# Leftover columns of a spectral layer as 32-row products, with its layer-norm statistics reordered

## The chip, the cores and the metric

The kernel runs on one core of a Trainium2 chip, as a single launch. The metric is device time in microseconds of that core, the median of several runs. The engines named below are TensorE (PE, with its weight loads shown as PEld), VectorE (DVE), ScalarE (ACT), GpSimd (POOL), and the DMA queues, which SyncE (SP) and POOL feed. All times are microseconds from the start of the profiled span unless marked ns.

## What is computed

The input `x` has 2048 rows of 576 columns in bf16. A spectral block is added to it, and then a gated feed-forward block:

```python
def _A_ref(x, w_r, w_i):
    B, S, D = x.shape
    X = rfft2(x.astype(float32), axes=(-2, -1))
    X = X * (w_r + 1j * w_i)
    return irfft2(X, s=(S, D), axes=(-2, -1)).astype(bfloat16)

def _B_ref(x, w_gate, w_up, w_down):
    return (gelu(x @ w_gate) * (x @ w_up)) @ w_down

x = A_x                                   # 1 x 2048 x 576
h = x + _A_ref(layernorm(x), A_w_r, A_w_i)
h2 = h + _B_ref(layernorm(h), B_w_gate, B_w_up, B_w_down)   # hidden width 4608
```

The change touches only the beginning of the spectral block: the first layer norm, and the part of the Fourier transform over rows and columns that comes first.

## The kernel before, in words

The 2048 rows stand as 16 tiles of 128 partitions (`h_sb[:, h, :]`, h from 0 to 15); row 16 p + h is partition p of tile h. The transform over the rows is split: first a product over the 128 partitions of each tile (length 128), later one that joins the 16 tiles. The transform over the columns is a product with tables of sines and cosines.

**Layer norm.** Each tile needs its mean and its 1/deviation. Eleven tiles are measured by DVE (`sd`: two `bn_stats` on halves of 288 columns, and a `bn_aggr` that joins them), five by ACT (`ln_act` on tiles 1, 3, 5, 9, 11: one pass that sums, one that sums squares, after which POOL's `ln_fin` subtracts the squared mean). POOL then makes `rstd` for groups of tiles (`ln_rstd`, L137 adds a small number, L138 raises to the power -1/2) and negative means (`minus_means`, L142, into `mneg`). DVE multiplies the row table `F16` by a tile's `rstd` (L391), which gives `FR[:, h]`. The mean is taken out by a further product with `mneg` as the weights.

**Row products.** For each tile, `row16` (L327, L334) makes six products on PE: columns 0 to 255 and 288 to 543 come out folded, that is as sums and differences of column n and column 288 + n, in a PSUM tile `f2t` that two tiles share. ACT copies it to `Bt[:, 0:4]` (`evict`, L361, one for two tiles). The columns that do not fit in these blocks, 256 to 287 and 544 to 575, are made by `rests` for four tiles at a time (`row16_rest`, L351): two products of 64 columns of `x` and two of the mean, which fill partitions 0 to 63 and 64 to 127 of one PSUM bank. Half of those 64 rows repeat columns that the blocks hold already, and the table `DF` has zeros there. `evict4` (L367) copies the bank to `Bt[:, 4]`, on ACT for tiles 0 to 7 and on DVE for 8 to 15.

**Column products.** `f2` (L550) then makes, for each of 16 groups of 128 row frequencies, six products: four with tables `DT` and two, for the leftovers, with `DF`. For the first group the two with `DF` stand last. They need all the evictions of all 16 tiles, so `f2` is the point where the opening ends. Behind it come `f3` (L567, L568), the product with the weights `WR` and `WI` on DVE, the inverse transforms (`i3`, `inv_cols`), the second layer norm, and the feed-forward block (L978 and L1021).

**The tables.** `DT` is made while the row products run: POOL makes angles (`kd`), DVE adds the phases (`phases`, L293, three of them) and drops the sign, ACT takes two sines (`col_sin`, L408), DVE mirrors them (L420) and copies rows of the third block into `DF` (L500, L501). The weights of the upper rows come by two indirect gathers on POOL (`gather`, L397) and a second transfer on SP (L504); `load_dq` (L518) rearranges `DT` into `DQ` for the inverse transform.

**Order.** Each engine works its queue strictly in the order in which the program issues; that order is written out by hand, from `for h in (1, 3, 5)` on, and no scheduler changes it. Tiles in PSUM come from one pool of four buffers of two banks that are handed round in order. Before the first row product PE multiplies an identity 12 times (`fill`, `FILL = {0: 12}`, L316), results that are overwritten. `sd` puts the `bn_aggr` of one tile between the two halves of the next (`flush`).

## Time and profile before

| What | Value |
|---|---|
| median of three runs | 494.85 us (494.26 to 495.02) |
| the profiled execution | 494.6 us, of which its span is 492.8 us |
| PE busy | 484.7 us, 98% of the span |
| DVE, ACT, POOL busy | 223.4, 158.2, 29.5 us |
| first slice of 12.3 us | PE 6 tenths, DVE 8, ACT 8, POOL 8 |
| first product of `f2` | 21.96 us |

The table of slices shows PE at nine tenths or more from the second slice to the next to last; only the first is lower. A row of the timeline reads: start, busy time from the first to the last of the merged instructions, engine, line, operation, what is written and read, shapes, and how many instructions were merged; a bracket tells how long the engine sat idle before and what released it. Busy times of matmuls include their way through the array, so products that follow each other overlap in these rows; the starts tell the pace.

### The profile page before, as it was taken

What the parts mean: (1) busy time and instruction counts of PE and PEld (TensorE: products, weight loads), DVE (VectorE), ACT (ScalarE), POOL (GpSimd) and SP (SyncE); (2) the same over time, 40 slices, a digit from 0 to 9 for tenths busy, and PEclk for the clock granted to TensorE, in tenths of its full rate; (3) what the DMA queues carried; (4) which work ended last, traced back from release to release, by engine and by line L of the source; (5) the groups of instructions that cost most, each with busy time, mean ns of one, the idle gap of its engine ahead of it and who ended that gap; (6) DMA issues with size and microseconds to landing.
All of it is one profiled execution on the core that took longest, in us unless ns stands there. A gap on an engine that the chain in (4) does not pass through costs nothing.

```text
span 492.8 us, 12868 instructions
## 1 busy us (share of the span) xinstructions
PE 484.7 (98%) x5762; PEld 338.9 (69%) x5762; DVE 223.4 (45%) x457; ACT 158.2 (32%) x280; POOL 29.5 (6%) x84
## 2 busy tenths in 40 slices
PE   6999999999999999999999999999999999999997
PEld 3777789875589955555699755555799655555995
DVE  8999774798622177333311345333121333333111
ACT  8899863322210022332200132332110232232000
POOL 8500010011100011000000000000000000000000
PEclk9999999999999999999999999999999999999999
DMA  8838979769970049966720089876600377760000
GB/s 278 234 74 184 246 115 240 165 128 212 223 161 3 3 118 195 192 145 147 152 65 1 37 170 199 174 145 147 143 3 3 92 158 155 150 146 1 14 13 25
DMA packets 89582, 62.35 MB, mean 127 GB/s; under 512 B 23222, under 2 KB 88118, under 8 KB 89526
## 3 DMA queue, kind: packets, MB, share of 16 engines
q1 hardware_dynamic: 89238, 60.34, 57.5%
q0 software_dynamic: 288, 1.18, 0.7%
q8 instruction: 45, 0.74, 0.7%
q14 instruction: 11, 0.09, 0.1%
HBM read 52.65 MB, written 2.36 MB: 112 GB/s over the span
## 4 chain that ended last, share of the span: by engine, by line
PE 95%; ACT 2%; POOL 1%; DMA 1%; issue 0%; DVE 0%; ACTq 0%; POOLq 0%
PE gu L978 57%; PE acc L1021 27%; PE pq_ps L550 2%; PE cs_ps L709 2%; PE acc L1040 2%; PE eo_ps L658 2%; ACT junk L128 1%; PE y_ps L848 1%; PE gh_ps L568 1%; PE gh_ps L567 1%; DMA h_sb<-in_A_x_dram 1%; POOL rstd L138 1%; ACT Bt L361 0%; POOL wm_r L397 0%; PE eo_ps L682 0%
## 5 line engine op out<-in xcount | busy, mean ns | idle before, releaser
L978 PE MATMUL gu<-Bt,wgu 64*128 64x512 bf16 (+1 forms) x2646 | 270.6, 363 | 0.0
L978 PEld LDWEIGHTS <-wgu 64*128 64x128 bf16 x2646 | 151.5, 94 | 115.6 <-issue 0.3
L987 DVE TENSOR_TENSOR P_sb<-g_sb,gu 128x512 bf16<-128x512 f32 (+1 forms) x156 | 100.4, 645 | 140.3 <-ACT g_sb L986 140.3
L986 ACT ACTIVATE g_sb<-gu 128x512 f32<-128x512 f32 (+1 forms) x156 | 88.0, 564 | 193.5 <-PE gu L978 193.5
L1021 PEld LDWEIGHTS <-P_sb 64*128 64x128 bf16 x2160 | 122.2, 94 | 10.9
L1021 PE MATMUL acc<-wd,P_sb 64*128 64x288 bf16 x1440 | 90.9, 283 | 0.0
L1030 DVE TENSOR_TENSOR part<-part,acc 128x576 f32<-128x576 f32 x15 | 11.3, 754 | 112.6 <-ACT part L1029 112.6
L1029 ACT COPY part<-acc 128x576 f32<-128x576 f32 x15 | 9.6, 639 | 122.8 <-PE acc L1021 122.8
L1021 PE MATMUL acc<-wd_a,P_sb 64*128 64x288 bf16 x720 | 46.8, 283 | 0.0
L550 PE MATMUL pq_ps<-DT,Bt 128*128 128x290 bf16 x64 | 12.3, 286 | 0.7 <-ACT Bt L361 0.7
L978 PE MATMUL gu<-Bt,wgu_e 64*128 64x256 bf16 (+1 forms) x162 | 12.5, 305 | 0.0
L873 DVE TENSOR_SCALAR hrow<-h_sb,mv,rstd 128x1152 bf16<-128x1152 bf16 x14 | 12.2, 868 | 0.6 <-POOL rstd L911 0.6
L138 POOL TENSOR_TENSOR rstd<-rstd,mhalf 128x1 f32<-128x1 f32 (+2 forms) x17 | 12.0, 709 | 1.4
L1032 DVE TENSOR_TENSOR h_sb<-h_sb,part 128x576 bf16<-128x576 bf16 x15 | 11.4, 758 | 0.5
L550 PEld LDWEIGHTS <-Bt 128*128 128x128 bf16 x96 | 9.1, 97 | 3.4 <-ACT Bt L361 0.8
L978 PEld LDWEIGHTS <-wgu_e 64*128 64x128 bf16 x162 | 10.3, 94 | 1.2
L137 POOL TENSOR_SCALAR rstd<-mv 128x1 f32<-128x1 f32 (+2 forms) x17 | 4.1, 242 | 116.7 <-DVE mv L123 116.0
L561 ACT CAST pq<-pq_ps 128x580 bf16<-128x580 f32 x16 | 10.5, 666 | 1.2 <-PE pq_ps L550 1.1
L709 PE MATMUL cs_ps<-DQ,EO 58*128 58x290 bf16 x144 | 10.8, 283 | 0.0
L327 PE MATMUL f2t<-FR,h_sb 128*128 128x256 bf16 x64 | 9.2, 273 | 0.6 <-DVE FR L391 0.6
L709 PEld LDWEIGHTS <-EO 58*128 58x128 bf16 x160 | 7.8, 94 | 2.4 <-issue 0.7
L550 PE MATMUL pq_ps<-DF,Bt 128*128 128x290 bf16 x32 | 8.9, 285 | 0.0
(149 smaller groups left out, 283.9 us busy)
## 6 DMA issues: line engine op xcount, KB each, us to landing
wgu<-in_B_w_gate_dram SPq DMA_DIRECT2D x46, 432.0 KB, 5.1
wgu<-in_B_w_up_dram SPq DMA_DIRECT2D x46, 432.0 KB, 6.1
wd_a<-in_B_w_down_dram SPq DMA_DIRECT2D x1, 1728.0 KB
wd<-in_B_w_down_dram SPq DMA_DIRECT2D x1, 1728.0 KB
wd<-in_B_w_down_dram SPq DMA_DIRECT2D x6, 288.0 KB, 7.9
out_dram<-h_sb SPq DMA_DIRECT2D x3, 576.0 KB
h_sb<-in_A_x_dram SPq DMA_DIRECT2D x4, 288.0 KB, 4.3
h_sb<-in_A_x_dram SPq DMA_DIRECT2D x2, 576.0 KB
```

Of the source, the lines that this page charges most:

```text
L138: G.tensor_tensor(dst[:, sl], dst[:, sl], mhalf[:, sl], ALU.pow)
L550: T.matmul(ps[:, par, 0:JP], lhsT=Bt[:, t, col], rhs=DT[:, t // 2, par] if t < 4 else DF[:, par], start=(t == par), stop=(t == 4),)
L561: copy(pq[c][:, rs].rearrange("p r (j a) -> p r j a", a=2), pq_ps[c][:, :, 0:JP].rearrange("p a (r j) -> p r j a", r=2)[:, rs],)
L658: T.matmul(pv[:, n], lhsT=z[:, a, w].rearrange("p b j -> p (b j)"), rhs=TI[:, ts[k], 1 - a : 3 - a, :], start=(a == 0), stop=(a == 1),)
L709: T.matmul(ps[:, e, 0:JP], lhsT=EO[x][rows, w, 2 * g : 2 * g + 2].rearrange("p h e k l -> p (h e k l)"), rhs=DQ[rows, w] if w or e else DT ...
L873: V.tensor_scalar(hrow[:], h_sb[:, h, :].rearrange("p (r k) -> p r k", k=64).unsqueeze(2).to_broadcast([P, NR, 2, 64]), mv2[:, h, 0:1], rs ...
L978: T.matmul(gu[:, c, 0:n], lhsT=w[rows, r, i * P : (i + 1) * P], rhs=hl[tcnk % 2][rows, r, lo:hi], start=(r == 0), stop=(r == NR - 1),)
L986: A.activation(g_sb, gu[:, 0, 0:n], ACT.Gelu_apprx_tanh)
L987: V.tensor_tensor(p_sb(f)[:, lo:hi], g_sb, gu[:, 1, 0:n], ALU.mult)
L1021: T.matmul(accs[i][:, c, 0:DH], lhsT=p_sb(f)[rows, st * P : (st + 1) * P], rhs=wd[f // NWA][rows, f % NWA, c * DH : (c + 1) * DH], start=( ...
L1030: V.tensor_tensor(part, part, accs[1][:, :, 0:DH], ALU.add)
L1032: V.tensor_tensor(hv, hv, part, ALU.add)
```

## The change

- The leftover columns are now packed without repeats. For each tile, `rests` makes four products of 32 columns of `x`, one for each 32 partitions of PSUM: the two runs of 32 leftover columns, each once for row frequencies 0 to 63 (partitions 0 to 63) and once for 64 to 127 (partitions 64 to 127). Two products of 64 rows take the mean out. Each product now has 64 columns instead of 128, and one PSUM bank holds eight tiles instead of four, so there are two `rests` and two `evict4` (the first on ACT, the second on DVE) instead of four.
- `DF` gets a second version: one has zeros in the partitions 64 to 127, the other in 0 to 63, and `f2` takes the one that belongs to its group of frequencies. The table's row numbers `iD` follow (three small `iota` instead of one), two DVE copies of 64 rows replace two of 32, and a part of the zeros is now set by POOL.
- The free half of `Bt[:, 4]` holds two constant rows (`edge`), which `load_dq` copies into `DQ` by two transfers more; the last piece of each `DT` transfer is two rows shorter.
- On ACT, tiles 1, 3 and 5 are measured by a first pass that yields the mean with a negative factor, and a second that takes it as a bias, so that it yields the variance at once; the two POOL operations of `ln_fin` are gone for these three. Factors in `neg` undo the scale in `minus_means`; two small memsets on DVE set them. The order of these passes changes, tiles 9 and 11 stay as they were.
- The order of the opening changes: the first gather stands before the `rstd` of tiles 4 to 7; `FR` and row products of tiles 0, 1 and 2, 3 stand between the statistics of tiles 6 and 7; the statistics of tiles 10 and 12 are split round the row products of 4 to 7 and the first `rests`; the second gather, the three phases, and the last aggregate move back. `FILL` goes from 12 to 9.

```diff
@@ -86,9 +86,9 @@
     nhpib = const("nhpib", -0.5 * PI)
     mhalf = keep.tile([P, H], FP32, name="mhalf")
     V.memset(mhalf[:], -0.5)
-    neg = keep.tile([P, 2], FP32, name="neg")
+    neg = keep.tile([P, 2, H], FP32, name="neg")
     for i in range(2):
-        V.memset(neg[:, i : i + 1], -2.0 + i)
+        V.memset(neg[:, i], -2.0 + i)
     mneg = keep.tile([P, 2, H], BF16, name="mneg")
 
 
@@ -108,7 +108,8 @@
 
     DT = keep.tile([P, 3, 2, 2, JH], BF16, name="DT")
     D3 = DT[:, 2]
-    DF = keep.tile([P, 2, 2, JH], BF16, name="DF")
+    DF = keep.tile([P, 2, 2, 2, JH], BF16, name="DF")
+    edge = Bt[0:2, 4, 8 * P : 8 * P + 4 * JH].rearrange("p (r a j) -> p r a j", r=2, a=2)
     DQ = keep.tile([P, NW, 2, JH], BF16, name="DQ")
     mv = keep.tile([P, H, 2], FP32, name="mv")
     rstd = keep.tile([P, H], FP32, name="rstd")
@@ -122,10 +123,21 @@
         V.bn_stats(st[:, 1, :], h_sb[:, h, DH:D])
         V.bn_aggr(dst[:, h, :], st[:])
 
-    def ln_act(h):
-        for i, fn, sc in ((0, ACT.Identity, 1.0 / D), (1, ACT.Square, 1.0 / D**0.5)):
-            junk = roll.tile([P, D], BF16, name="junk", tag="junk", bufs=2)
-            A.activation(junk[:], h_sb[:, h, :], fn, scale=sc, accum_out=mv[:, h, i : i + 1])
+    ROOT = float(D) ** 0.5
+
+    def act_pass(h, i, fn, scale, bias=0.0):
+        junk = roll.tile([P, D], BF16, name="junk", tag="junk", bufs=2)
+        A.activation(junk[:], h_sb[:, h, :], fn, bias=bias, scale=scale, accum_out=mv[:, h, i : i + 1])
+
+    def act_mean(h):
+        act_pass(h, 0, ACT.Identity, -1.0 / (D * ROOT))
+
+    def act_var(h):
+        act_pass(h, 1, ACT.Square, 1.0 / ROOT, mv[:, h, 0:1])
+
+    def act_sums(h):
+        act_pass(h, 0, ACT.Identity, 1.0 / D)
+        act_pass(h, 1, ACT.Square, 1.0 / ROOT)
 
     def ln_fin(hs):
         sq = roll.tile([P, H], FP32, name="sq", tag="sq", bufs=2)
@@ -142,7 +154,7 @@
         G.tensor_tensor(
             mneg[:, :, lo:hi],
             mv[:, lo:hi, 0].unsqueeze(1).to_broadcast(sh),
-            neg[:].unsqueeze(2).to_broadcast(sh),
+            neg[:, :, lo:hi],
             ALU.mult,
         )
 
@@ -185,7 +197,7 @@
     def iota(t, pattern, base=0, cm=0):
         G.iota(t, pattern=pattern, base=base, channel_multiplier=cm, allow_small_or_imprecise_dtypes=True)
 
-    V.memset(DF[:], 0.0)
+    V.memset(DF[64:128, 0], 0.0)
     V.memset(DT[:, :, 1, :, JH - 1], 0.0)
 
     iu, ic = tmp("iu", [P, H, 8]), tmp("ic", [P, H, 8])
@@ -204,7 +216,8 @@
     make_identity(nc, ident[:])
     iD = tmp("iD", [P, 3], FP32)
     iota(iD[:], [[P, 3]], 0, 1)
-    iota(iD[64:128, 2:3], [[0, 1]], 2 * P + 64 + 192, 1)
+    for p0, d0 in ((32, 544), (64, 256), (96, 544)):
+        iota(iD[p0 : p0 + 32, 2:3], [[0, 1]], d0, 1)
     iJ = tmp("iJ", [P, 2 * JM], FP32)
     iota(iJ[:], [[1, 2], [2, JM]])
     iDs = tmp("iDs", [P, 3], FP32)
@@ -308,7 +321,7 @@
         V.tensor_scalar(F16[:, 1, :], F16[:, 0, :], -1.0, None, op0=ALU.mult)
 
     ps_f = {}
-    FILL = {0: 12}
+    FILL = {0: 9}
 
     def fill(dst, n):
 
@@ -339,21 +352,27 @@
                 stop=True,
             )
 
-    def rests(h):
-        ps_f["f4", h] = two("f4")
-        for i in range(4):
-            row16_rest(h + i)
-
-    def row16_rest(h):
-        o = (h % 4) * P
-        for mean in (False, True):
-            for p0, d0 in ((0, 256), (64, 512)):
+    def rests(h0):
+        ps = ps_f["f4", h0] = two("f4")
+        for h in range(h0, h0 + 8):
+            o = (h - h0) * 64
+            for x in range(2):
+                for n in range(2):
+                    p0, d0 = 64 * x + 32 * n, 256 + DH * n
+                    T.matmul(
+                        ps[p0 : p0 + 32, 0, o : o + 64],
+                        lhsT=h_sb[:, h, d0 : d0 + 32],
+                        rhs=FR[:, h, 0, 64 * x : 64 * x + 64],
+                        start=True,
+                        stop=False,
+                    )
+            for x in range(2):
                 T.matmul(
-                    ps_f["f4", h - h % 4][p0 : p0 + 64, 0, o : o + P],
-                    lhsT=mneg[:, 1, h : h + 1].to_broadcast([P, 64]) if mean else h_sb[:, h, d0 : d0 + 64],
-                    rhs=FR[:, h, 0, :],
-                    start=not mean,
-                    stop=mean,
+                    ps[64 * x : 64 * x + 64, 0, o : o + 64],
+                    lhsT=mneg[:, 1, h : h + 1].to_broadcast([P, 64]),
+                    rhs=FR[:, h, 0, 64 * x : 64 * x + 64],
+                    start=False,
+                    stop=True,
                 )
 
     def evict(*hs):
@@ -364,9 +383,9 @@
             )
 
     def evict4(h):
-        (V.tensor_copy if h >= 8 else A.copy)(
-            Bt[:, 4, :].rearrange("p (c h l) -> p h c l", c=16, h=16)[:, h : h + 4, :, :],
-            ps_f["f4", h][:, 0].rearrange("p (h c l) -> p h c l", h=4, c=16),
+        (V.tensor_copy if h else A.copy)(
+            Bt[:, 4, 0 : 8 * P].rearrange("p (c h l) -> p h c l", c=8, h=H)[:, h : h + 8],
+            ps_f["f4", h][:, 0].rearrange("p (h c l) -> p h c l", h=8, c=8),
         )
 
     agg = []
@@ -380,11 +399,19 @@
 
 
         for h in hs:
-            st = roll.tile([P, 2, 6], FP32, name="st", tag="st", bufs=3)
-            V.bn_stats(st[:, 0, :], h_sb[:, h, 0:DH])
+            lower(h)
             flush()
-            V.bn_stats(st[:, 1, :], h_sb[:, h, DH:D])
-            agg.append((h, st))
+            upper(h)
+
+    half = {}
+
+    def lower(h):
+        half[h] = roll.tile([P, 2, 6], FP32, name="st", tag="st", bufs=3)
+        V.bn_stats(half[h][:, 0, :], h_sb[:, h, 0:DH])
+
+    def upper(h):
+        V.bn_stats(half[h][:, 1, :], h_sb[:, h, DH:D])
+        agg.append((h, half[h]))
 
     def norms(lo, hi):
         for h in range(lo, hi):
@@ -434,90 +461,99 @@
                     stop=True,
                 )
 
-    for h in (1, 3, 5):
-        ln_act(h)
+    act_mean(1)
+    act_mean(3)
+    act_var(1)
+    act_var(3)
+    act_mean(5)
     row_table()
     sd(0)
     minus_row()
     sd(2, 4)
     small_table()
-    ln_fin(slice(1, 4, 2))
     ln_rstd(rstd, mv, 0, 4)
-    minus_means(0, 4)
     angle_b(first)
     angle_s(first)
     angle_c(first)
+    for i in range(2):
+        V.memset(neg[:, i, 1:6:2], (2 - i) * ROOT)
+    minus_means(0, 4)
+    gather(0)
     sine(first)
+    act_var(5)
     cosine(first)
     A.activation(G16v[0], pt[0][:, 0, 0 : 2 * P], ACT.Copy, scale=G_SCALE)
     for h in (9, 11):
-        ln_act(h)
-    sd(6, 7)
+        act_sums(h)
+    sd(6)
+    norms(0, 2)
+    sd(7)
+    norms(2, 4)
     flush()
-    ln_fin(slice(5, 6))
     ln_rstd(rstd, mv, 4, 8)
     minus_means(4, 8)
-    gather(0)
-    norms(0, 4)
-    rests(0)
     minus_sine(first)
     turn_tf(first)
-    sd(8, 10)
+    sd(8)
+    lower(10)
     flush()
     norms(4, 8)
-    rests(4)
+    rests(0)
+    upper(10)
+    lower(12)
+    flush()
     ln_fin(slice(9, 12, 2))
     ln_rstd(rstd, mv, 8, 12)
     minus_means(8, 12)
+    evict(0, 2, 4, 6)
+    evict4(0)
+    upper(12)
+    sd(13)
+    flush()
     gather(1)
-    evict(0, 2)
-    evict4(0)
-    evict(4, 6)
-    evict4(4)
-    sd(12, 13)
-    flush()
     ln_rstd(rstd, mv, 12, 14)
     minus_means(12, 14)
-    phases(0)
     norms(8, 12)
-    rests(8)
     sd(14, 15)
+    norms(12, 14)
     flush()
     ln_rstd(rstd, mv, 14, 16)
     minus_means(14, 16)
-    norms(12, 14)
-    phases(1, 2)
+    phases(0, 1, 2)
     drop_sign(kd[:], pd[:])
     norms(14, 16)
-    rests(12)
+    rests(8)
+    G.memset(DF[0:64, 1], 0.0)
+    for r, a, v in ((0, 0, 1.0), (0, 1, -1.0), (1, 0, 0.0), (1, 1, 0.0)):
+        G.memset(edge[:, r, a], v)
     evict(8, 10)
     col_sin(1, pd, zerob)
     col_sin(0, kd, hpib)
     evict(12, 14)
     mirror(1)
     mirror(0)
+    for x in range(2):
+        V.tensor_copy(DF[64 * x : 64 * x + 64, x], D3[64 * x : 64 * x + 64])
     evict4(8)
-    V.tensor_copy(DF[0:32], D3[0:32])
-    V.tensor_copy(DF[96:128], D3[96:128])
-    evict4(12)
     for w, t in ((WR, wm[0]), (WI, wm[1])):
         nc.sync.dma_start(w[:, 9 : H + 1, 0:J], t[:].rearrange("p (r j) -> p r j", r=8))
     angle_a(rest)
     angle_b(rest)
     for w in (WR, WI):
         G.tensor_scalar(w[:, :, 0 : J : J - 1], w[:, :, 0 : J : J - 1], 0.5, None, op0=ALU.mult)
-        if w is WR:
-            for z in Zts:
-                G.memset(z[:].rearrange("p a w b j -> p (a w b) j")[:, :, JW:], 0.0)
+    for z in Zts:
+        G.memset(z[:].rearrange("p a w b j -> p (a w b) j")[:, :, JW:], 0.0)
     def load_dq(r):
         for w in range(1 - r, NW):
             j0, j1 = w * JW, (w + 1) * JW
-            for lo, hi in ((j0, min(j1, (j0 // P + 1) * P)), ((j0 // P + 1) * P, j1)):
+            for lo, hi in ((j0, min(j1, (j0 // P + 1) * P)), ((j0 // P + 1) * P, min(j1, DH))):
                 if lo < hi:
                     p0 = 64 * r + lo - j0
                     nc.sync.dma_start(
                         DQ[p0 : p0 + hi - lo, w], DT[lo % P : lo % P + hi - lo, lo // P, :, r, :]
                     )
+        p0 = 64 * r + DH % JW
+        nc.sync.dma_start(DQ[p0 : p0 + 2, NW - 1], edge[:, r])
 
     load_dq(1)
 
@@ -549,8 +585,8 @@
         for par, t in steps:
             T.matmul(
                 ps[:, par, 0:JP],
-                lhsT=Bt[:, t, col],
-                rhs=DT[:, t // 2, par] if t < 4 else DF[:, par],
+                lhsT=Bt[:, t, col if t < 4 else slice(col.start % (8 * P), col.start % (8 * P) + P)],
+                rhs=DT[:, t // 2, par] if t < 4 else DF[:, slot[c] // 8, par],
                 start=(t == par),
                 stop=(t == 4),
             )
```

## The prediction

> **What bounds the kernel now.** I read the page's head and chain first, then the chain in order of time, then each engine's timeline up to 25 us.
>
> ```profile
> span 492.8 us, 12868 instructions
> PE 95%; ACT 2%; POOL 1%; DMA 1%; issue 0%; DVE 0%; ACTq 0%; POOLq 0%
> ```
>
> TensorE (PE) is 95% of the chain that ends last. The change adds and removes nothing after the first column product `f2`, whose 96 products keep their shape (only half of the `DF` operand is zeros). So the question is when `f2` can start and go on. The chain in order of time ends the opening so:
>
> ```profile
> 18.00 1.06 POOL rstd L138
> ...
> 19.43 0.67 ACT DT L408
> 20.10 1.82 ACT Bt L361 x2
> 21.96 2.46 PE pq_ps L550 x18
> ```
>
> GpSimd (POOL) makes the last `rstd`, ScalarE (ACT) the column tables and the last two evictions, and then PE runs. PE's own timeline:
>
> ```profile
> 9.76 0.38 PE L327 MATMUL f2t<-FR,h_sb 128*128 128x256 bf16 x2 [0.57 <-DVE FR L391]
> ...
> 12.61 0.39 PE L327 MATMUL f2t<-FR,h_sb 128*128 128x256 bf16 x2
> ...
> 14.76 0.22 PE L334 MATMUL f2t<-FR,mneg 128*128 128x128 bf16 x1
> 14.91 0.25 PE L351 MATMUL f<-FR,h_sb 128*64 128x128 bf16 x2
> ...
> 15.33 0.22 PE L351 MATMUL f<-FR,mneg 128*64 128x128 bf16 x2
> 15.48 0.39 PE L327 MATMUL f2t<-FR,h_sb 128*128 128x256 bf16 x2
> ...
> 20.50 0.22 PE L334 MATMUL f2t<-FR,mneg 128*128 128x128 bf16 x1
> ...
> 22.52 0.42 PE L550 MATMUL pq_ps<-DF,Bt 128*128 128x290 bf16 x2
> ```
>
> The 16 products of one `rests`, 128 columns each, go in eight concurrent pairs; from the first pair at 14.91 to the eighth at 15.33 are seven steps, a little under 0.06 each. A row tile (`row16`) takes 0.55: four from 12.61 to 14.82, its last product being one such step from 14.76. On either side stands a gap: 14.76 to 14.91 and 15.33 to 15.48 are 0.15, where 0.055 would do inside a run of one shape. The whole `rests` occupies 15.48 - 14.82 = 0.66, of which 8 x 0.056 = 0.45 is work (a row tile is ten such steps of 128 columns, 0.55), so **one change of tile shape costs 0.11**. The row at 22.52 is where `f2` first uses the leftovers; that start is what I compare.
>
> **The opening, queue by queue.** VectorE (DVE):
>
> ```profile
> 7.64 0.45 DVE L384 BATCH_NORM_STATS2 st<-h_sb 128x6 f32<-128x288 bf16 x1
> ...
> 9.35 0.21 DVE L377 BATCH_NORM_AGGREGATE mv<-st 128x2 f32<-128x12 f32 x1
> 9.47 0.82 DVE L391 TENSOR_SCALAR FR<-F,rstd 128x256 bf16<-128x256 bf16 x4
> ...
> 12.11 0.92 DVE L391 TENSOR_SCALAR FR<-F,rstd 128x256 bf16<-128x256 bf16 x4
> ...
> 14.95 0.87 DVE L391 TENSOR_SCALAR FR<-F,rstd 128x256 bf16<-128x256 bf16 x4
> 15.74 0.45 DVE L384 BATCH_NORM_STATS2 st<-h_sb 128x6 f32<-128x288 bf16 x1
> ...
> 17.37 0.21 DVE L377 BATCH_NORM_AGGREGATE mv<-st 128x2 f32<-128x12 f32 x1
> 17.56 0.48 DVE L391 TENSOR_SCALAR FR<-F,rstd 128x256 bf16<-128x256 bf16 x2
> 17.95 0.65 DVE L293 SCALAR_TENSOR_TENSOR pd<-iJ,iD,kd 128x146 f32<-128x146 f32 x2
> 18.64 0.39 DVE L232 TENSOR_SCALAR kd<-pd 128x438 int32<-128x438 int32 x1
> 19.10 0.48 DVE L391 TENSOR_SCALAR FR<-F,rstd 128x256 bf16<-128x256 bf16 x2
> ...
> 21.77 0.69 DVE L367 CAST Bt<-f 128x512 bf16<-128x512 f32 x1
> ```
>
> Two tiles' statistics cost 1.63 (15.74 to 17.37), a half 0.36 or a little more; four `FR` 0.8, two 0.4. POOL:
>
> ```profile
> 9.72 0.27 POOL L137 TENSOR_SCALAR rstd<-mv 128x4 f32<-128x4 f32 x1 [0.48 <-DVE FR L391]
> 10.07 1.26 POOL L138 TENSOR_TENSOR rstd<-rstd,mhalf 128x4 f32<-128x4 f32 x1
> ...
> 13.87 1.05 POOL L138 TENSOR_TENSOR rstd<-rstd,mhalf 128x4 f32<-128x4 f32 x1
> ...
> 15.28 1.13 POOL L397 DMA_INDIRECT wm_i<-in_A_w_i_dram,rev  x1 [0.18 <-issue]
> ...
> 16.80 0.72 POOL L138 TENSOR_TENSOR rstd<-rstd,mhalf 128x2 f32<-128x2 f32 x1
> ```
>
> **The change, part by part.** Tiles 4 to 7: `FR` 0 to 3 now stand ahead of the statistics of tile 7, and two small memsets are new, so the aggregate of 7 moves from 9.35 to 9.35 + 0.8. POOL, which waited for it, ends the power at 10.07 + 0.8 + 1.26 = 12.13; DVE is there sooner. `FR`(4) stays at 12.1 (before 12.11).
>
> Tiles 8 to 11: after four `FR` (to 12.95) come the halves of 10 and 12, so tile 10 is aggregated at 13.7 to 13.9. The power started 0.3 after its addition and lasts 1.05 (13.87): 13.9 + 0.3 + 1.05 = 15.25. `FR`(8) 15.25, before 14.95.
>
> Tiles 12, 13: two statistics 15.25 + 0.8 + 1.6 = 17.65. POOL: gather(1) 0.36 after the power (14.92 to 15.28), 15.6 to 16.75; addition and 0.72 of power give 17.85. `FR`(12) 17.85, before 17.56.
>
> Tiles 14, 15: tile 15's aggregate, formerly at 17.37 and ahead of `FR`(12), now follows `FR`(13): 17.85 + 0.4 = 18.25, which is 0.88 later. The power (18.00 in the chain) moves to 18.88 and ends at 19.94. `FR`(14) 19.97, before 19.10: **0.87 later**. The three phases (two took 0.68 with their tail, the third adds 0.28) end near 19.3, with `drop_sign` 19.7; the column sines can't run before. PE began tile 14 0.35 after its `FR` (it ended tile 15 at 20.55, two tiles of 0.55 later); so tile 14 starts at 20.32 and **tile 15 ends at 21.42**; before it ended at 20.50 + 0.05.
>
> Leftover products. Each tile now needs four 32-row products of 64 columns and two 64-row ones; per tile the shape changes twice. The nearest price is the 0.11 above, for 128 against 64; no row shows 32 against 64. Bounds: nothing, or 0.11 each. Streams are half as long, 0.028 if a group runs at once. One `rests` of eight has 17 changes and 16 groups: 17 x 0.11 + 16 x 0.028 = **2.3**, or 2 x 0.11 + 0.45 = **0.67** without a price inside. I take 2.3, because another pair of small shapes also shows the gap:
>
> ```profile
> 63.07 1.22 PE L917 MATMUL pt<-ident,hflat 128*64 128x128 bf16 x36
> 64.22 1.35 PE L848 MATMUL y_ps<-cs,G 64*128 64x288 bf16 x16
> ```
>
> Eighteen pairs of 0.056 end at 64.07; the next shape starts at 64.22, 0.15 later. [...]
>
> First `rests`: tiles 4 to 7 end on PE at 12.1 + 0.3 + 4 x 0.55 = 14.6; then 16.9 instead of 15.27. Tiles 8 to 13 end at 16.9 + 6 x 0.55 = 20.2, still before `FR`(14) lets 14 start at 20.32. So the first block is covered by that wait, just. Second `rests`: on the path. It ends at 21.42 + 2.3 = 23.72. Its last products are complete about 0.1 after that, DVE's eviction takes 0.69 (21.77) and 0.05 to PE: leftovers usable at 24.55. Before: 22.52. **Sum +2.0.**
>
> ACT: one eviction fewer, the ten statistics passes stay ten and keep their order of cost; a bias from a tile I price at 0 (bounds 0 and ±0.1 in all; ACT's sines use tile biases already).
>
> ```profile
> 11.53 1.90 ACT L361 CAST Bt<-f2t 128x1024 bf16<-128x1024 f32 x2
> ...
> 16.57 0.59 ACT L367 CAST Bt<-f 128x512 bf16<-128x512 f32 x1 [0.54 <-PE f L351]
> ...
> 18.86 0.68 ACT L408 ACTIVATE DT<-pd,zerob 128x438 bf16<-128x438 f32 x1
> ```
>
> The first eviction stays at 11.53, behind the passes, so the earlier `FR`(0) buys nothing. The 0.59 + 0.54 of the second leftover eviction go, but ACT then waits for tile 9 on PE (18.2): evictions of 8 and 10 to 20.1, sines to 21.25, 12 and 14 to 23.2. That is inside 23.72; it sets the start if the leftovers are cheap. DVE's eviction fewer, 0.69, lies in DVE's wait for PE. `DF` copies over 64 instead of 32 partitions have the same length and the same cover.
>
> At nothing: gather(0) earlier (POOL waits for tile 7 then), two more iotas (`ln_fin`'s two operations go ahead of the same `rstd`), the POOL memsets (after the last mean, before it waits for `WR`). SP gets two more small `DQ` transfers in a queue that had let eleven of them and then weights go by 37.9; `DQ` is first read at 47.95:
>
> ```profile
> 37.90 0.70 SPq L159 DMA_DIRECT2D wgu<-in_B_w_gate_dram  x1
> 47.95 0.80 PE L709 MATMUL cs_ps<-DQ,EO 58*128 58x290 bf16 x9
> ```
>
> Profiled execution: 494.6 with span 492.8; median 494.85, 0.25 above. 494.6 + 2.0 = **496.6**. About 0.2%, 1 us, is what a measurement can tell from no change.
>
> **The rivals.** *A, forecast*: every change between 32 and 64 rows drains: 496.6. Chance 0.58, with its own range 495.9 to 497.2 (power 0.72 or 1.06, drain 0.09 to 0.13).
>
> *B, not slower*: the four 32-row products and the following pair share the array with no drain. Place: inside `rests`. Then ACT decides: tile 15 complete at 21.6, eviction of 14 to 22.65, four products of `f2` later 23.2: +0.7, 495.3. For it: eight pairs of one width run without gaps. Against it: both width changes shown cost 0.11. The leftovers are usable at 22.25 plus the price of one `rests`, so +1.0 is passed at 1.25, that is (1.25 - 0.45) / 17 = 0.05 per change. Chance 0.22.
>
> *C, cold PE*: three fill products fewer.
>
> ```profile
> 4.05 5.14 PE L316 MATMUL f2t<-h_sb,ident 128*128 128x512 bf16 x12
> ```
>
> ```profile
> L316 PE MATMUL f2t<-h_sb,ident x12: 474/634/634, 4.1 to 8.7; 128*128 128x512 bf16 x12
> ```
>
> Twelve fills in 5.14 are 0.43 each for 512 columns, half the pace of the pairs above (four steps of 0.056); only the last, at 8.7, is shorter. So PE ran slow until about 8.9, some 5 after it began. Nine fills end at 7.9; `FR`(0), behind tile 6's statistics, comes at 8.55, and PE follows 0.3 later (9.47 to 9.76), so it idles from 7.9 to 8.85. If that restarts the wait of 5, speed comes at 14.0: 4.7 tiles at 1.1, 3.3 at 0.55, so tile 7 ends at 15.8 instead of 14.6, and after `rests` tile 14 starts at 21.4 instead of 20.32: +3.1, 497.7. [...] Chance 0.15.
>
> *D, faster*: the DVE time saved lets the later tables come sooner and closes small PE waits behind `f2`. DVE's queue alone holds `FR`(14) past 19, so the opening can't give 1 us: 493.6 needs something I don't see. Chance 0.05.
>
> **How the numbers follow.** Likeliest is A: 496.6. The range drops D and the ends of B and C: 495.1 to 497.7. Slower by over 0.2%: most of A, C, a little of B, 0.71; within: most of B, some of A, 0.24; faster 0.05.
>
> **What would show it.** In the new trace: one `rests` of eight lasting 2.3 or 0.7; gaps of about 0.13 between 32- and 64-row products; `FR`(14) near 20.0; the first use of `DF` near 24.55; the fills' pitch and the speed of tiles 0 to 3. I am wrong if the tile widths share the array without a gap, or if PE waits behind `f2` shrink by as much as its start slips.

## The result, and the profile after

The changed kernel takes 497.18 us (median of six runs, 497.07 to 497.66) and the kernel before 494.73 beside it (494.21 to 495.06): a ratio of 1.0053, with a 95% interval of 1.004 to 1.0066. It is **2.45 us slower**, half a per cent, and the interval keeps clear of 1. The forecast was 496.6 in a range of 495.1 to 497.7.

The profiled execution of the changed kernel took 497.44. Its page, the span and the chain that ended last, by engine:

```profile
span 495.7 us, 12929 instructions
PE 96%; DVE 1%; DMA 1%; ACT 1%; POOL 0%; SPq 0%; issue 0%
```

The span is 2.9 longer. PE's timeline of the changed kernel (columns as before: start, busy time, engine, line, operation; in brackets the idle time and what ended it):

```profile
4.05 4.02 PE L329 MATMUL f2t<-h_sb,ident 128*128 128x512 bf16 x9
8.81 0.58 PE L340 MATMUL f2t<-FR,h_sb 128*128 128x256 bf16 x2 [0.74 <-DVE FR L418]
...
9.30 0.63 PE L340 MATMUL f2t<-FR,h_sb 128*128 128x256 bf16 x2
...
12.84 0.38 PE L340 MATMUL f2t<-FR,h_sb 128*128 128x256 bf16 x2
...
14.98 0.22 PE L347 MATMUL f2t<-FR,mneg 128*128 128x128 bf16 x1
15.13 0.21 PE L362 MATMUL f<-FR,h_sb 128*32 128x64 bf16 x4
15.27 0.22 PE L370 MATMUL f<-FR,mneg 128*64 128x64 bf16 x2
15.42 0.21 PE L362 MATMUL f<-FR,h_sb 128*32 128x64 bf16 x4
...
17.32 0.22 PE L370 MATMUL f<-FR,mneg 128*64 128x64 bf16 x2
17.47 0.39 PE L340 MATMUL f2t<-FR,h_sb 128*128 128x256 bf16 x2
...
21.81 0.22 PE L347 MATMUL f2t<-FR,mneg 128*128 128x128 bf16 x1
21.96 0.21 PE L362 MATMUL f<-FR,h_sb 128*32 128x64 bf16 x4
...
24.15 0.22 PE L370 MATMUL f<-FR,mneg 128*64 128x64 bf16 x2
24.30 0.67 PE L586 MATMUL pq_ps<-DT,Bt 128*128 128x290 bf16 x4
25.16 0.42 PE L586 MATMUL pq_ps<-DF,Bt 128*128 128x290 bf16 x2 [0.19 <-DVE Bt L386]
```

Read the starts. Inside a block of leftovers the four 32-row products begin at 15.13, the two 64-row products at 15.27, the next tile's at 15.42: a step of 0.145 at every change of shape. The row tile in front ends at 14.98 + 0.055 = 15.04, the next begins at 17.47, so the block lasts 2.43 where the old one of half as many tiles took 0.66. The second block stands right before `f2`, and the first use of `DF` moves from 22.52 to 25.16, by 2.64. The first four row tiles run at half pace: 0.63 for a pair up to 12.5, then 0.38; the clock record of this trace has full speed from 12.63 on.

The rest of the opening, on DVE and on POOL:

```profile
19.61 0.64 DVE L418 TENSOR_SCALAR FR<-F,rstd 128x256 bf16<-128x256 bf16 x2
24.41 0.69 DVE L386 CAST Bt<-f 128x512 bf16<-128x512 f32 x1 [1.23 <-PE f L370]
```

```profile
18.72 0.86 POOL L150 TENSOR_TENSOR rstd<-rstd,mhalf 128x2 f32<-128x2 f32 x1
19.53 0.57 POOL L526 MEMSET DF<- 64x580 bf16 x1
```

The last two `FR` take 0.64 instead of 0.48, beside a POOL memset that was not there before. And DVE's last eviction waits for PE, as PE's products wait for nothing.

The first product of the feed-forward block, in the kernel before and then in the changed kernel:

```profile
65.31 6.93 PE L978 MATMUL gu<-Bt,wgu 64*128 64x256 bf16 x123
```

```profile
67.87 4.31 PE L1014 MATMUL gu<-Bt,wgu 64*128 64x256 bf16 x75
```

From there to the end of the span it is 492.81 - 65.31 = 427.50 before and 495.66 - 67.87 = 427.79 now. So 2.56 of the longer span arises before the feed-forward block, and 0.29 at the end.

### The profile page after: what moved, and what is told of

Its sections match the earlier page's. It is cut to its first block, busy times and chain, and to the rows that moved or that the text cites. A ratio compares the mean times of both kernels' runs of the same rounds, so it can differ in the third digit from the quotient of the medians.

```text
span 495.7 us, 12929 instructions
## 1 busy us (share of the span) xinstructions
PE 487.6 (98%) x5791; PEld 343.2 (69%) x5791; DVE 223.1 (45%) x458; ACT 158.1 (32%) x279; POOL 31.2 (6%) x87
## 4 chain that ended last, share of the span: by engine, by line
PE 96%; DVE 1%; DMA 1%; ACT 1%; POOL 0%; SPq 0%; issue 0%
PE gu L1014 57%; PE acc L1057 27%; PE cs_ps L745 2%; PE acc L1076 2%; PE f2t L340 2%; PE pq_ps L586 2%; PE eo_ps L694 2%; PE y_ps L884 1%; DMA h_sb<-in_A_x_dram 1%; PE gh_ps L604 1%; PE gh_ps L603 1%; PE f L370 0%; PE f L362 0%; PE f2t L347 0%; PE eo_ps L718 0%; PE pt L953 0%
## 5 line engine op out<-in xcount | busy, mean ns | idle before, releaser
L1014 PE MATMUL gu<-Bt,wgu_e 64*128 64x256 bf16 (+1 forms) x162 | 12.5, 305 | 0.0
L340 PE MATMUL f2t<-FR,h_sb 128*128 128x256 bf16 x64 | 10.8, 305 | 0.7 <-DVE FR L418 0.7
```

The costliest lines, as they stand in the source:

```text
L340: T.matmul(f2t[:, b, t * 2 * P : (t + 1) * 2 * P], lhsT=x[:, d0 : d0 + P], rhs=FR[:, h] if n else plus, start=(n == 0), stop=False,)
L1014: T.matmul(gu[:, c, 0:n], lhsT=w[rows, r, i * P : (i + 1) * P], rhs=hl[tcnk % 2][rows, r, lo:hi], start=(r == 0), stop=(r == NR - 1),)
```

## Experiments

All times are medians; in brackets the kernel before on the same chip, then the ratio with its 95% interval. Since the chips differ by some tenths, an experiment is compared by its distance to its own kernel before.

**1. One shape inside the block.** The mean is taken out by four 32-row products, so that the eight products of a tile all have one shape. Once with 9 fills (first), once with 12 (second); a third run has the 12 fills alone.

```diff
             for x in range(2):
-                T.matmul(ps[64 * x : 64 * x + 64, 0, o : o + 64],
-                    lhsT=mneg[:, 1, h : h + 1].to_broadcast([P, 64]), ...)
+                for n in range(2):
+                    p0 = 64 * x + 32 * n
+                    T.matmul(ps[p0 : p0 + 32, 0, o : o + 64],
+                        lhsT=mneg[:, 1, h : h + 1].to_broadcast([P, 32]), ...)
```

```diff
-    FILL = {0: 9}
+    FILL = {0: 12}
```

> The changed kernel, with the mean taken out by four products of 32 rows per tile in place of two of 64: eight products per tile, all of one shape, the same result. Theory drain (each change between 32- and 64-row products costs 0.11 to 0.13 us): one block of leftovers falls from 2.43 to about 0.7 us (two changes at its ends, 16 groups of four at 0.03), the first use of DF comes at 22.7 to 23.0 instead of 25.16, and the time falls by 2.2 us, to about 495.0. Rival, the 32-row products themselves are slow (0.05 us each, one after the other): with eight per tile a block takes about 3 us and the time rises to about 498.

> Both edits, 32-row means and 12 fills. If the drain is most of the loss and the clock matters only while TensorE is the bound, this is no faster than the first edit alone (within 0.2 us, about 494.9): the norms of tiles 14 and 15 then set the end. If the clock counts by itself, it is 0.5 to 0.7 us below it, about 494.4.

> The changed kernel with 12 fill products instead of 9. Theory cold clock (the missing fills let TensorE idle from 8.1 to 8.8 us, so it ran slow up to 12.5): row tiles 0 to 3 run at 0.55 each from the start, tile 4 starts near 12.2 instead of 12.84, and the first use of DF comes 0.5 to 0.7 us earlier, 496.5. Rival, the slow tiles 0 to 3 are covered by the statistics: no change, 497.2.

Measured: one shape 495.64 [494.32; 1.0028, 1.0018 to 1.0039]; one shape and 12 fills 495.45 [494.32; 1.002, 1.0011 to 1.0029]; 12 fills alone 497.08 [494.32; 1.0067, 1.0054 to 1.0081]. PE's timeline of the version with both:

```profile
14.34 0.22 PE L347 MATMUL f2t<-FR,mneg 128*128 128x128 bf16 x1
14.49 0.21 PE L362 MATMUL f<-FR,h_sb 128*32 128x64 bf16 x4
14.53 0.20 PE L372 MATMUL f<-FR,mneg 128*32 128x64 bf16 x4
14.56 0.20 PE L362 MATMUL f<-FR,h_sb 128*32 128x64 bf16 x4
...
14.96 0.22 PE L372 MATMUL f<-FR,mneg 128*32 128x64 bf16 x4
...
22.64 0.67 PE L588 MATMUL pq_ps<-DT,Bt 128*128 128x290 bf16 x4 [0.49 <-ACT Bt L382]
23.14 0.41 PE L588 MATMUL pq_ps<-DF,Bt 128*128 128x290 bf16 x2
```

There are more products than in the changed kernel (64 instead of 48 in a block), and the steps fall from 0.145 to 0.03; from the first to the last start it is 0.47 instead of 2.19. The way in keeps its 0.15, and the way out is not free either: in the mended packing of experiment 4 the next row tile starts 0.22 after the last of these starts (14.93 to 15.15). `f2` then waits for ACT's last eviction and not for the leftovers. With 9 fills too: there the first use of `DF` comes at 23.27 and not at the 22.7 to 23.0 expected, and the time is 0.6 above the 495.0 expected. With 12 fills on both sides, one shape saves 497.08 - 495.45 = **1.63**. Fewer fills cost nothing that the medians show: 497.08 with 12 lies 2.76 above its kernel before, the changed kernel with 9 lay 2.45 above. (Experiment 5 repeats this.)

**2. Each half of the change alone.** First the new order and the new statistics with the old leftovers (four blocks of 64-row pairs, the old `DF`, 9 fills); then the packing alone, in the order, with the statistics and the 12 fills of before.

```diff
     norms(4, 8)
     rests(0)
+    rests(4)
...
-    rests(8)
+    rests(8)
+    rests(12)
```

```diff
     norms(4, 8)
-    rests(4)
+    rests(0)
...
-    rests(12)
+    rests(8)
```

> The new order and the new statistics with the old leftovers (64-row products of 128 columns, four tiles to a block, the old DF). Theory: the order by itself costs, since FR of tile 14 stays at 19.6 us, 0.5 later than before, and two blocks stand behind tile 15: first use of DF near 23.2, about 495.4. Rival, the order is free or a gain and all of the loss is the packing: 494.7 or below.

> The packing alone (32-row products, two blocks of eight tiles, the two versions of DF, the new rows of DQ) in the order, statistics and 12 fills of the kernel before. Theory drain: two blocks of 2.43 us on TensorE; tile 8 starts near 17.0, tile 15 ends near 21.4, first use of DF near 24.6 (before 22.52), 2.1 us slower than before. Rival, the new order causes most of the loss: within 0.7 us of before.

Measured: the order alone 495.94 [494.32; 1.0032, 1.0019 to 1.0044], the packing alone 496.9 [494.53; 1.005, 1.0036 to 1.0063]. Together the two distances would make 1.62 + 2.37 = 3.99, and the change as a whole costs about 2.4: they overlap. The chain of the order alone, in order of time (start, length, what), shows where its own price comes from:

```profile
19.51 0.29 DVE FR L410
...
19.85 0.39 PE f2t L338 x2
...
21.12 0.59 PE f L362 x16
21.73 0.69 DVE Bt L378
22.42 0.21 DVE DF L528
22.64 0.31 DVE DF L529
22.98 0.70 DVE Bt L378
```

Two old blocks now stand behind the last tile, and their two evictions and the `DF` copies follow one another on DVE, up to a first use of `DF` at 23.73. With the packing there is one such block and one eviction. This is also why the order alone came out above the 495.4 expected, which had the first use at 23.2. So the 1.6 of the order alone is not what the order costs in the changed kernel; experiment 4 comes nearer to that. The packing alone has its first use of `DF` at 24.55, with the same 2.43 for each block: it carries most of the loss by itself.

**3. The packing with one shape and the memset moved.** As the packing alone, with the mean in 32-row products, `G.memset(DF[0:64, 1])` early on POOL (after the iota of `rev`), and the four small memsets of `edge` late.

```diff
     iota(rev[:], [[0, 1]], 2 * P - 1, -2)
+    G.memset(DF[0:64, 1], 0.0)
...
     rests(8)
-    G.memset(DF[0:64, 1], 0.0)
```

> The packing in the order of before, with the mean taken out by 32-row products, and the zeros of DF set by GpSimd early (behind rev) and the edge rows late (behind the scaling of WI), so that no memset runs beside FR of tile 14. Theory: blocks of 0.73 us, FR of tile 14 at 19.1 as before and 0.29 us long, tile 15 ends near 20.6, first use of DF 22.2 to 22.5, 0 to 0.3 us faster than before. Rival, the leftovers cost in some other way (more products, the two copies of 64 rows, two more transfers): 0.5 us slower or more.

Measured: 495.51 [494.53; 1.0019, 1.001 to 1.0028]. 1.39 less than the packing alone, but still 0.98 above the kernel before. Three things were left. The memset still stood beside work of DVE, only earlier:

```profile
6.89 0.60 DVE L272 TENSOR_SCALAR pr<-pr 128x256 int32<-128x256 int32 x1
```

```profile
6.77 0.57 POOL L269 MEMSET DF<- 64x580 bf16 x1
```

The same operation on DVE takes 0.28 in the kernel before. The input also landed 0.10 later in this execution, and together they move every table behind: `FR`(0) comes at 9.90 instead of 9.47, `FR`(14) at 19.51 instead of 19.10. So moving the memset moved its price to another DVE operation. Then, in this profile PE pauses twice within tile 8, 0.19 before 16.25 and 0.26 before 16.95, for nothing that the profile shows, while POOL's second gather runs; ACT stands idle for 0.98 before 17.22 there too, and `f2` starts late because ACT's last eviction is late. What holds PE there stays open. And from the feed-forward block's first product to the end it is 427.8, not 427.5, as in every version with the packing up to here, and unlike the order alone (427.5).

**4. What else the packing costs.** In the traces each of SP's transfers names one of eight semaphores (101 to 107 and 109) for its end, in turn, and others wait for it. There are 152 transfers in the kernel before and 154 after the change, so the two added `DQ` transfers shift all later ones. The last transfer of the output has semaphore 109 in the kernel before, which SP's closing list waits for last, and 102 after the change, which the list waits for first; the five other waits, 0.06 each, then come behind it. To restore the count without touching the packing, the last weight matrix is loaded in four transfers instead of six:

```diff
-    for i, bk in enumerate((17, 21, 25, 29, 33, 35)):
-        todo.setdefault(bk, []).append((load_wd2, slice(2 * i, 2 * i + 2)))
+    for i, bk in enumerate((17, 22, 28, 33)):
+        todo.setdefault(bk, []).append((load_wd2, slice(3 * i, 3 * i + 3)))
```

This edit alone, on the changed kernel; and then, with it, two versions with one shape in the block, 12 fills, and the zeros of `DF` written by ACT in an early pause instead of by POOL: one in the order and with the statistics of before, one in the new order with the new statistics. The four small memsets of `edge` stand late in both.

```diff
     A.activation(fs[:], mu[:].rearrange("p c l -> p (c l)"), ACT.Sin, ...)
+    A.copy(DF[0:64, 1].rearrange("p a b j -> p (a b j)"), zerob[0:64, 0:1].to_broadcast([64, 4 * JH]))
...
-    G.memset(DF[0:64, 1], 0.0)
```

> The changed kernel with the last weight matrix loaded in four transfers instead of six, and nothing else: as many SP transfers as the kernel before. Theory (the two added transfers shift which semaphore the last output transfer gets, so that it is waited for first and five waits come after it): last product to end 3.26 instead of 3.54, so 0.28 us below the changed kernel. Rival (the longer tail comes from something else in the packing): tail stays at 3.54 and the time with it.

> The kernel before (its order, statistics and 12 fills) with the packing alone, the mean removed by four 32-row products per tile (one shape inside a block), the zeros of DF written by ACT right after its first sine instead of by POOL, the four small memsets of the edge late, and the last weight matrix in four transfers instead of six, so that the number of transfers is that of the kernel before. My theory (drain, memset beside DVE's tables, and the rotation of the transfers' semaphores are all that the packing costs): first use of DF 22.2 to 22.4, from the first product of the gate to the end 427.5 instead of 427.8, so 0 to 0.3 us below the kernel before. Rival (the packing has a price of its own beyond these): at least 0.3 us above the kernel before.

> The changed kernel (its order and statistics) with 12 fills, four 32-row mean products, the zeros of DF written by ACT early, the edge late, and the last weight matrix in four transfers. Theory: the table of tile 14 takes 0.29 instead of 0.58 and the first use of DF is at about 22.85, 0.3 above the kernel before, which with the tail as before gives before + 0.3 to 0.5 us: the price of the order by itself. Rival (the memset and the tail are not what the version with 32-row means still lost): as that version, before + 1.1 us.

Measured: the changed kernel with as many transfers as before 496.98 [494.27; 1.0049, 1.0035 to 1.0063]; the packing so mended 494.42 [494.27; 1.0002, 0.9993 to 1.0011]; the whole change so mended 494.66 [494.27; 1.0008, 0.9999 to 1.0017].

The end first. In all three the span from the first product of the feed-forward block is 427.50 again (496.12 - 68.62 in the first of them). What SP waits for at its end, in the changed kernel and then with the four transfers (engine, line, what it waited for: total, times, longest):

```profile
SPq L1131 <- DMA out_dram<-h_sb: 1.2, 1, 1.2
```

```profile
SPq L1131 <- DMA out_dram<-h_sb: 0.9, 1, 0.9
```

The last transfer has semaphore 109 again. So the 0.29 at the end is shown in the spans, and it belongs to the number of transfers. The median of the first did not fall with it: 2.71 above its kernel before, against 2.45 and 2.32 (below) without the edit, where 0.28 less was expected. Its profiled execution lost 1.3 elsewhere (experiment 5), and single executions of the changed kernel scatter over two microseconds, so five runs don't resolve 0.28.

Then the memset. The chain in the version with one shape and POOL's memset (experiment 1), where `FR`(14) runs beside the memset, has

```profile
19.63 0.59 DVE FR L420
20.26 0.39 PE f2t L340 x2
```

against 0.29 and a start of PE 0.34 after it in the order alone (above), which has no memset at that place. With the zeros written by ACT it is again

```profile
20.33 0.48 DVE L421 TENSOR_SCALAR FR<-F,rstd 128x256 bf16<-128x256 bf16 x2
```

for both `FR`, and PE follows 0.34 later, at 20.67. From `FR`(14) to the start of `f2` it is 3.01 with POOL's memset (19.63 to 22.64) and 2.71 without (20.33 to 23.04), so the memset is worth 0.30 in these traces. In absolute times the second trace is the later one, with the first use of `DF` at 23.55 where 22.85 was expected: DVE stood idle for 1.40 up to 6.73 until a part of the input had landed, while in the first trace it didn't wait there at all. That profiled execution took 495.3, against the median of 494.66.

By the medians this version lies 0.39 above its kernel before, the one with POOL's memset and the longer end 1.13: the two were worth 0.74 together, against 0.30 + 0.29 in the traces. That leaves **0.39 for everything else, the new order and statistics among it**, with an interval that just reaches zero. Against the mended packing in the old order, on the same chip, the new order and statistics cost 494.66 - 494.42 = 0.24, which these runs can't tell from nothing.

The packing so mended equals the kernel before; it does not beat it, although its first use of `DF` comes at 22.08, 0.44 earlier. Its PE timeline tells where that went:

```profile
22.08 0.41 PE L560 MATMUL pq_ps<-DF,Bt 128*128 128x290 bf16 x2
...
25.94 0.41 PE L560 MATMUL pq_ps<-DT,Bt 128*128 128x290 bf16 x2 [0.21 <-ACT g L599]
```

The same product began at 26.02 in the kernel before, so of the lead only 0.08 is left. ACT's `g` stands behind a sine, ACT's `TF`, which waits for DVE's angles `pr`. DVE in the mended packing, its POOL beside it, and DVE in the kernel before:

```profile
22.02 1.15 DVE L248 SCALAR_TENSOR_TENSOR pr<-q,s2p,ks 128x896 int32<-128x896 f32 x1
23.21 1.08 DVE L272 TENSOR_SCALAR pr<-pr 128x896 int32<-128x896 int32 x1
```

```profile
22.21 1.22 POOL L514 TENSOR_SCALAR WR<-WR 128x34 bf16<-128x34 bf16 x1 [3.37 <-DMA WR<-wm_r]
23.31 0.49 POOL L517 MEMSET Zt<- 128x120 bf16 x3
```

```profile
22.50 1.15 DVE L245 SCALAR_TENSOR_TENSOR pr<-q,s2p,ks 128x896 int32<-128x896 f32 x1
23.68 0.63 DVE L269 TENSOR_SCALAR pr<-pr 128x896 int32<-128x896 int32 x1
```

The first angle operation ends 0.48 earlier, but then the second takes 1.08 instead of 0.63, beside POOL's memsets, which POOL itself began late: its product of 34 columns took 1.22 beside DVE's operation, where the kernel before has 0.41. The lead is lost between DVE and POOL, not on PE.

**5. The clock.** The changed kernel once more, without an edit; again with 12 fills; and with its second block issued twice over into the same sums (the values stay the same):

```diff
-    def rests(h0):
+    def rests(h0, times=1):
...
-        for h in range(h0, h0 + 8):
+        for h in list(range(h0, h0 + 8)) * times:
...
-    rests(8)
+    rests(8, 2)
```

> The changed kernel as it is, beside the next one on the same chip. If the 9 fills let the clock open late in a part of the executions, its times scatter by 0.5 us or more, with the low ones near those of 12 fills.

> The changed kernel with 12 fills. Theory cold clock: 0.3 to 0.6 us below the one beside it in the median (not in all executions). Rival: no difference in the median.

> The changed kernel with the second block of leftover products (tiles 8 to 15) issued twice over, into the same sums: 16 tiles with 32 more changes of shape, and the same values. Both theories: the block lasts 4.8 us instead of 2.43, the first use of DF is 2.33 later. Theory (a stretch of products with a drain at each counts as idle for the clock, in windows of 3.41 us that run on from the opening): with 4.8 us of block and 0.2 of wait every position of the windows leaves one nearly filled with drains, so the clock record shows 0.5 for about 3.4 us in nearly every execution, the profiled one too, and the median is 497 + 2.3 + 1.3 (what the closed window cost where it was seen) = 500.6. Rival (the two closings seen had another cause, or come at random): no closing in most executions, 497 + 2.3 = 499.3.

Measured: again 496.85 [494.53; 1.0048, 1.0034 to 1.0061], of which the profiled execution took 498.6; with 12 fills 497.31 [494.53; 1.0052, 1.0038 to 1.0066]; with the block twice 500.83 [494.26; 1.0124, 1.0107 to 1.0142]. So again 12 fills gain nothing.

The profiled execution of the repeat is 1.8 above the others, and the reason stands in its busy time by windows (from:to, length, busy of PE with its instructions, of PEld, DVE, ACT, POOL; then the granted clock of PE, the DMA share, GB/s):

```profile
14.76:18.17 3.41, 3.41 (x61) 2.65 (x60) 2.98 (x12) 1.69 (x3) 3.11 (x6) 1.00 0.92 100
21.58:25.00 3.42, 3.23 (x56) 2.06 (x55) 1.92 (x7) 1.89 (x3) 0.58 (x2) 1.00 0.77 224
25.00:28.41 3.41, 3.41 (x15) 2.14 (x16) 2.96 (x4) 1.95 (x3) 0.67 (x6) 0.50 0.20 45
```

From 25.00 to 28.41 PE gets half its clock (0.50), just behind the second block, and `f2` runs its first products at half pace (0.24 from start to start, 0.12 at full clock). The same stands in the changed kernel with four transfers, from 24.86 to 28.28. It costs 1.3: from the first use of `DF` to the first product of the feed-forward block it is 44.07 and 44.08 in these two, 42.71 in the first profile of the changed kernel. The other three profiles with mixed blocks, that is with a change of shape inside every tile (12 fills twice, the packing alone), don't have it. In the records of the clock, full speed came at 7.93 and 7.80 in the two; 25.00 and 24.86 are five times 3.41 later. In the kernel before and in the first profile of the changed kernel the stretch at full clock (8.90 to 493.60 and 12.63 to 497.33, as the record runs on past the span) lasts 484.69, which is 142 times 3.413. So in these records the clock changed at whole multiples of 3.41 after the start of full speed, below called windows, and where they lie against the block differs from execution to execution.

The executions without a profile have their mean granted clock on record. One window at half clock in 497 us makes 0.9966 by reckoning, and the two profiles with one such window stand at 0.996. Of the 31 executions with the mixed block once, four stand at 0.996: two with 12 fills (498.29 and 498.35), one of the repeat (498.6) and one with four transfers (497.9), the last two being the profiles above. They took 0.9 to 1.8 longer than the median of the others of their run. Where in the two without a profile the clock fell is not recorded. None of the 58 executions of the versions without mixed blocks, and none of the kernel before beside them, is below 0.999.

The same view with the block doubled:

```profile
13.51:16.92 3.41, 3.41 (x61) 2.54 (x59) 3.18 (x13) 2.09 (x3) 2.85 (x5) 1.00 0.96 168
20.34:23.75 3.41, 3.41 (x60) 2.55 (x59) 1.60 (x6) 2.82 (x4) 0.95 (x5) 1.00 1.00 297
23.75:27.16 3.41, 3.22 (x56) 2.15 (x55) 0.90 (x2) 0.00 (x0) 0.84 (x6) 1.00 0.22 50
27.16:30.58 3.42, 3.42 (x16) 2.15 (x15) 2.83 (x4) 2.22 (x3) 0.00 (x0) 0.50 0.10 21
```

Full speed came at 6.68, six windows before 27.16. The first two windows shown hold 2.4 us of block each and are followed by full speed; the third holds 2.37 of block, the wait of 0.19 for the leftovers, and is followed by half speed. The median lies 6.57 above its kernel before; the changed kernel, in its two measurements, 2.45 and 2.32. The difference is 4.1 to 4.3, where 2.33 of further block alone would give 2.3 and a closed window on top 3.6. Four of the five executions have a clock of 0.992 to 0.997 (0.992 is more than one window); the fifth, at full clock, was the fastest with 499.73. So with the block doubled four of five executions have a lower clock, where with the single block it was four of 31. That the lower clock goes with the mixed blocks is shown by this; that the time at the changes of shape counts as idle was the author's theory, which fits but is not shown, and only one of the five executions has a profile. The execution at full clock is 5.47 above the kernel before, where 2.4 and 2.33 make 4.7, so about 0.7 besides is not accounted for.

## Why the prediction came out right, point by point

**The drain** (rival A, the forecast): right in place and size. 2.3 was taken for a block, 2.43 measured; a change costs 0.145 from start to start, where a step inside one shape takes 0.03, so 0.115 against the 0.11 taken. That longer step is what the rows show; what PE does in it they do not. The condition named for rival B, products of these widths that share the array without a gap, held only where they all have one shape, and then a block with its entry and exit takes 0.78 (14.37 to 15.15 in the mended packing), against the 0.67 of the text. The step from there to the end held too: 1.6 by the prediction's two block lengths, 1.63 between the medians. That the two agree so closely is partly luck: with 9 fills the distances differ by 2.45 - 1.32 = 1.13, on two chips, and the two profiled executions with 12 fills are 1.24 apart at the start of the feed-forward block (67.20 and 65.96).

**`FR`(14) 0.87 late**: half wrong, with an error on each side. It came at 19.61, only 0.51 late, as the last power began 0.16 earlier than reckoned and took 0.86 and not 1.06; but it took 0.3 longer beside the new POOL memset. That these two errors of about 0.3 nearly cancel in the sum is luck. "At nothing: ... the POOL memsets" looked at who waits for POOL, and not at who works beside it.

**The first block covered by the wait for `FR`(14)**: right where PE was at speed by then. In the version with four transfers tile 13's last product starts at 19.96 and tile 14 at 20.14, later by 0.12 than one step. In the first profile PE was late, and tile 14 followed at once, at 20.77.

**First use of `DF` at 24.55**: 25.16 in the first profile, and 24.96, 24.75, 24.64, 24.54 in four other profiles of it (as it is, twice with 12 fills, and with four transfers). The first is high because full speed came only at 12.63.

**The `DF` copies**: of the same length, as priced: the two of 64 partitions took 0.62 together in the changed kernel, the two of 32 before 0.29 and 0.31.

**ACT's bias "at 0"**: too low, without effect on the sum. Three passes take 0.76 instead of 0.67, and the first eviction starts at 11.74 instead of 11.53; ACT later waits 1.33 for PE.

**"Nothing after the first column product"**: wrong by 0.29, the end. The two transfers were priced by when their data is read. It is the largest term that the sum lacked in every profile, and with it the 2.0 becomes 2.3, against 2.45 and 2.32 between the medians.

**Rival C**: the idle time after the fills does not show in the medians, so it was right not to take it. But a late full speed exists: by the clock records it came at 12.63 in the first profile, at 6.68 to 7.93 in the other five with 9 fills, and at 6.49 to 9.65 in the eight with 12. It cost the first profile about 0.5 (25.16 against 24.64). Whether the idle time caused it there, one profile can't show.

**Rival D**: it didn't come; where `f2` did come earlier (experiment 4), an engine behind PE took the gain back.

From 12 fills with the change, the loss of 2.76 splits into 1.63 for the changes of shape, 0.74 for the memset and the end, and 0.39 for the rest, order and statistics among it. The sum closes because each term is the difference of two neighbours, each taken against its own kernel before; the last one is barely above nothing.

## What to carry to other kernels

Small products packed into PE were cheap here only in a row of one shape (0.03 from start to start, 0.145 at a change): look at the starts at each change, and rather issue more products of the same shape than fewer of two. Price a small operation on POOL also by the DVE operations that run beside it (`FR` took 0.59 instead of 0.29), and a transfer added anywhere also by the order in which the end waits (0.29 for two). And before a gain in one stage is booked, find who waits next in the following stage: here 0.44 us were gone 4 us later.

## What was not expected of the hardware

- **The clock fell again without a long pause.** Behind windows of 3.41 us with 2.2 to 2.4 us of mixed block and a wait of 0.19, PE got half its clock (0.50) for a whole window, at a cost of 1.3; behind windows with 2.4 of block and no wait it did not. It fell five and six times 3.41 after full speed, and PE's rows show no gap over 0.19 in the windows before. The packing alone, with 2.15 of block and the same wait in one window, kept its speed; what made the difference was not measured.
- **DVE and POOL operations took longer beside each other**: `FR` took 0.59 instead of 0.29 and DVE's short `pr` 0.60 instead of 0.28 beside a memset, the long `pr` 1.08 instead of 0.63, POOL's operation on 34 columns 1.22 instead of 0.41. The first three are `tensor_scalar`, and the last stood beside a `scalar_tensor_tensor`; why the times rose no run here shows.
- **The end of the kernel changed with the number of transfers before it**: 0.29 for two more, gone with two fewer.
